# Two-layer block after attention: the channel matrix decoded in the token stage, and layer 1's tensor-tensor work on VectorE

## The chip, the cores and the metric

The kernel runs on one core of a Trainium2 chip. Its engines are TensorE (PE in the views; PEld is its loading of weights), VectorE (DVE), ScalarE (ACT), GpSimd (POOL) and SyncE (SP), which here issues the transfers. The metric is the device time of one execution in microseconds, as the median of several.

## The reference

Three layers in a row, for 4 batches of 448 tokens and 768 channels:

```
attn_out = attention with two 12x12 mixings of the heads      # 4 x 12 x 448 x 64
x = attn_out as (batch, 448, 768)
# layer 1
h = gelu(x @ w_in);  u, v = halves of h                       # 512 columns each
v_n = (v - mean) / sqrt(var + 1e-6) * g_ln
gated = u * (w_sg @ v_n + b_sg)                               # over tokens
x = x + gated @ w_out
# layer 2
theta = x @ w_theta
y = w_tok_r @ (x * cos(theta)) + w_tok_i @ (x * sin(theta))   # over tokens
u = x + y
out = u + relu(u @ w_ch)
```

The weight matrices `w_in`, `w_out`, `w_theta`, `w_tok` and `w_ch` arrive as 64-bit floating-point words.

## The kernel before

Attention takes the first half of the time, in 180 blocks of ten rows and twelve heads. Then two dense layers follow, `moe1` and `moe2`. All their products run in a 32-bit format of reduced precision, three per product: each operand is kept as a high part (a cast, on ScalarE) and a low part (the difference between value and cast, `rest`), and high x high, high x low and low x high are added up in PSUM.

A 64-bit weight has first to be decoded into such a pair. A decode job does it for 128x256 words in six steps: load the raw words (SyncE), *words* (two activations on ScalarE; a shift L602 and a bit operation L604 on VectorE), *value* (a mask, L610, VectorE), *high* (a cast on ScalarE and a product, L618), *low* (a difference L624 and a sum L625, both GpSimd), *store* to DRAM. `tick` issues one step each of several jobs, a later step for an older job. In layer 1 the jobs for `w_out` stay on the chip (tiles named wout); those of `w_theta`, `w_tok` and `w_ch` go to DRAM and are loaded again as pairs when layer 2 needs them. The last 18 jobs are those of `w_ch`.

The order of the work is written out by the kernel itself: a list of *units*, each the products for one PSUM bank, and what stands before and after each unit (`pre`, `post`). Each engine runs its instructions in that order. Units of layer 1 are value chunks (`v_chunk`, 3 or 4 per batch), `out` (6 per batch), `u_half` (4) and `gate` (4). The tables TV, TU, TG and TO say how many ticks stand behind each unit of each kind. The E_ tables choose VectorE (V) or GpSimd (P) for differences and products: of x (E_X), of the normalised v (E_VN), of the gate (E_G), the gate's own product (E_GM), and the product in the decode (E_MV).

In layer 2 a *theta* unit makes half a chunk of angles; `angles` (five instructions on VectorE, three on ScalarE) makes cosine and sine, `rotate` multiplies x by them (two or four on VectorE) and splits the results into z (cast on ScalarE, difference on GpSimd). When the four chunks of batch 0 and the first of batch 1 are through, six token units (`tok`, some 84 products each) follow, each with the addition of x on VectorE (L1092), a cast on ScalarE and a difference on GpSimd (u). Then theta for the rest of batch 1, then six channel units (`ch`) with `w_ch`, and so on through the batches. PSUM is a pool of eight banks that the units take in turn; a transposed x also takes a bank.

Of the kernel before, what the change touches and what calls it, by code (L numbers as in the profile page):

```python
# [18 lines left out]
DM = H * D  # L19
# [458 lines left out]
NO2 = 3  # L478
E_MV = 'PVPPV'
E_X = ('VVVPPP', 'VPVVVP', 'VVPVPP', 'VVVPPP')  # L480
E_VN = ('PPV', 'PPP', 'PPV', 'PVV')
E_GM = ('VVVV', 'VVVV', 'VVVP', 'VVVV')
E_G = ('PPPV', 'VVPP', 'VPVP', 'VVPV')
TV = ((0, 1, 3, 1), (2, 2, 2, 2), (2, 1, 2, 2), (0, 1, 2, 0))
TU = ((2, 1, 0, 1), (2, 0, 2, 1), (2, 0, 2, 1), (3, 0, 2, 1))
TG = ((1, 0, 1, 0), (2, 1, 0, 1), (0, 1, 0, 1), (0, 1, 0, 0))
TO = ((2, 1, 1, 0, 1, 1), (0, 1, 0, 0, 2, 0), (0, 1, 1, 0, 0, 1), (0, 1, 1, 3, 2, 2))
KE = 1
# [8 lines left out]
class Dense:  # L497


    def __init__(self, tc, nc, io, xT, x2T, outT):  # L500
        self.tc, self.nc, self.io = tc, nc, io
        self.xT, self.x2T, self.outT = xT, x2T, outT
        self.pools, self.psum = {}, None
        self.units, self.before, self.after, self.at = [], {}, {}, 0
        self.jobs, self.job_at = [], 0
        self.raw_bufs, self.mid_bufs, self.out_bufs = 1, 1, 1
        self.const = {}
        self.made = 0

# [41 lines left out]

    def eng(self, c):
        return self.nc.vector if c == "V" else self.nc.gpsimd


# [10 lines left out]
    def scratch(self, dram):  # L566
        t = lambda name, r, c: dram.tile([2, r, c], F32, name=name)
        self.win_d = t("win_d", DM, DFF)
        self.wth_d = t("wth_d", DM, DM)
        self.wtok_d = t("wtok_d", 2 * S, S)  # L570
        self.wch_d = t("wch_d", DM, DM)

    def decode(self, src, n, dst, tiles=None):
# [39 lines left out]
        def high(pool):  # L613
            h = block(pool, 0)
            nc.scalar.activation(out=h, in_=box["a"], func=AF.Copy)
            self.made += 1
            eng = self.eng(E_MV[self.made % len(E_MV)]) if not tiles else nc.vector
            eng.tensor_tensor(out=box["p"], in0=box["p"], in1=box["low"], op=ALU.mult)  # L618
            box["h"] = h

        def low(pool):
            a, p, h = (box[k] for k in ("a", "p", "h"))
            lo = block(pool, 1)
            nc.gpsimd.tensor_tensor(out=a, in0=a, in1=h.bitcast(F32), op=ALU.subtract)  # L624
            nc.gpsimd.tensor_tensor(out=lo, in0=a, in1=p, op=ALU.add)  # L625
            box["lo"] = lo
# [37 lines left out]
def moe1(d, left, right):  # L664
# [6 lines left out]
    def start():  # L671
# [21 lines left out]
        for k in range(KF):  # L693
            def tiles(k=k):
# [52 lines left out]
    def split_x(b, k):  # L747
        if k == 0:
            xt[b] = ([], [])
        raw = res.pop(("x", b, k))  # L750
        n = 512 if b % 2 == 0 else S
        h, l = (d.pools["x"].tile([128, 512], F32R, tag=f"x{i}{k}", name="x") for i in range(2))
        d.cast(h[:, :n], raw[:, :n])
        d.rest(d.eng(E_X[b][k]), l[:, :n], raw[:, :n], h[:, :n])
        xt[b][0].append(h)
        xt[b][1].append(l)
# [33 lines left out]
    def norm_split(b, c):  # L790
        v = vraw.pop((b, c))
        if c < 3:
            hi, lo = (d.pools["vn"].tile([128, HF], F32R, tag=f"vn{c}{i}", name="vn") for i in range(2))
            d.cast(hi, v)
            d.rest(d.eng(E_VN[b][c]), lo, v, hi)
            vn[b, c] = (hi, lo)
        else:
            for e in range(2):
                m = d.pools["vn"].tile([128, HF], F32R, tag=f"vnm{e}", name="vnm")
                p, o = slice(64 * e, 64 * e + 64), slice(64 - 64 * e, 128 - 64 * e)  # L800
                d.cast(m[p], v[p])
                d.rest(nc.gpsimd, m[o], v[p], m[p])
                mixed[b + e] = (m, p)
# [16 lines left out]
    def gate(b, f):  # L820
# [6 lines left out]
        for c in range(3):  # L827
# [120 lines left out]
def moe2(d, left, win_es, last_u, m1_left):  # L948
# [301 lines left out]
```

## Time and profile before

| | us |
|---|---|
| median of 3 runs | 1045.97 |
| lowest and highest | 1043.34, 1046.72 |
| the profiled execution, its own time | 1047.47 |
| its span | 1045.6 |
| attention ends and layer 1 begins | about 484 to 531 |
| layer 1 ends, theta begins | 748.3 |
| batch 0's token units begin, end | 785.5, 811.9 |

The span is what the views show; 1.9 us of the execution lie outside it. Times in the views count from the span's start. A lower number in the column of the granted clock (PEclk) means that TensorE ran part of that stretch at 1.2 GHz in place of 2.4. In a row of the timeline the bracket tells how long the engine was idle before and what released it; in a row of grouped lines "mean ns" is the mean length of one instruction.

### The profile page before, as it was taken

What the parts mean: (1) busy time and instruction counts of PE and PEld (TensorE: products, weight loads), DVE (VectorE), ACT (ScalarE), POOL (GpSimd) and SP (SyncE); (2) the same over time, 40 slices, a digit from 0 to 9 for tenths busy, and PEclk for the clock granted to TensorE, in tenths of its full rate; (3) what the DMA queues carried; (4) which work ended last, traced back from release to release, by engine and by line L of the source; (5) the groups of instructions that cost most, each with busy time, mean ns of one, the idle gap of its engine ahead of it and who ended that gap; (6) DMA issues with size and microseconds to landing.
All of it is one profiled execution on the core that took longest, in us unless ns stands there. A gap on an engine that the chain in (4) does not pass through costs nothing.

```text
span 1045.6 us, 21830 instructions
## 1 busy us (share of the span) xinstructions
PE 982.3 (94%) x7848; PEld 742.7 (71%) x7848; DVE 775.5 (74%) x1458; ACT 586.6 (56%) x1374; POOL 622.4 (60%) x818
## 2 busy tenths in 40 slices
PE   7789999999999999997978999799999999999998
PEld 2445655565656555566756979587888999999997
DVE  2799878987888878985989998898896724925611
ACT  4577778786777778775754645454364412613310
POOL 0596558754686548854656877775666643753622
PEclk9899999999999999998989999999999999999999
DMA  5757565556556564347353676758956131130021
GB/s 191 154 167 221 142 139 183 180 168 129 161 193 203 131 158 152 131 108 265 113 155 89 213 225 199 229 188 274 335 184 226 41 106 31 32 106 16 31 76 53
DMA packets 135504, 159.47 MB, mean 153 GB/s; under 512 B 30309, under 2 KB 120933, under 8 KB 135397
## 3 DMA queue, kind: packets, MB, share of 16 engines
q1 hardware_dynamic: 135397, 158.08, 50.3%
q8 instruction: 63, 1.03, 0.4%
q14 instruction: 44, 0.36, 0.1%
HBM read 86.66 MB, written 32.85 MB: 114 GB/s over the span
## 4 chain that ended last, share of the span: by engine, by line
PE 57%; DVE 20%; DMA 9%; POOL 5%; issue 4%; ACT 3%; SPq 1%; DVEq 0%; ACTq 0%; POOLq 0%
PE ps L564 27%; PE psB L223 10%; PE psA L203 5%; PE psD L329 5%; DVE da L604 3%; PE psC L280 3%; PE psC L277 3%; DMA blk<-s 2%; PE psC L278 2%; DVE pl L262 2%; DVE da L602 2%; DVE dp L610 2%; DMA xres<-xT 2%; DVE dp L618 2%; DMA xraw<-xT 1%
## 5 line engine op out<-in xcount | busy, mean ns | idle before, releaser
L255 POOL TENSOR_SCALAR ph<-e,rc 120x448 f16<-120x448 f32 x180 | 163.9, 911 | 147.3 <-DVE rc L250 99.8
L223 PE MATMUL psB<-blk,kpre 120*120 120x448 f32 x360 | 177.3, 575 | 13.0 <-DMA blk<-s 8.2
L229 DVE TENSOR_REDUCE nmx<-psB 120x1 f32<-120x448 f32 x180 | 111.3, 618 | 49.9 <-PE psB L223 40.8
L262 DVE SCALAR_TENSOR_TENSOR pl<-e,rc,ph 120x448 f16<-120x448 f32 x180 | 147.4, 819 | 0.0
L236 ACT ACTIVATE e<-psB,nmx 120x448 f32<-120x448 f32 x180 | 114.3, 635 | 43.1 <-DVE nmx L229 43.0
L308 DVE SCALAR_TENSOR_TENSOR al<-psC,ah 128x480 f16<-128x480 f32 x180 | 116.1, 645 | 8.2 <-ACT ah L302 7.9
L277 PE MATMUL psC<-wh,ph 120*128 120x120 f16 x720 | 97.7, 218 | 10.9 <-DVE al L308 7.1
L302 ACT ACTIVATE ah<-psC 128x480 f16<-128x480 f32 x180 | 103.0, 572 | 7.6 <-PE psC L280 4.9
L209 ACT ACTIVATE s<-psA 120x896 f32<-120x896 f32 (+1 forms) x90 | 82.5, 917 | 42.5 <-PE psA L203 41.1
L564 PE MATMUL ps<-wtok,z 128*128 128x448 f32 x504 | 104.8, 368 | 0.4 <-POOL z L560 0.4
L564 PEld LDWEIGHTS ps<-wtok,z 128*128 128x128 f32 x504 | 94.4, 188 | 10.1 <-POOL z L560 0.8
L277 PEld LDWEIGHTS <-ph 120*128 120x128 f16 x720 | 68.8, 99 | 44.3 <-issue 18.6
L278 PE MATMUL psC<-wl,ph 120*128 120x120 f16 x720 | 97.1, 218 | 2.4 <-issue 2.4
L329 PEld LDWEIGHTS <-ah 128*128 128x128 f16 x1536 | 76.6, 99 | 31.2 <-issue 31.2
L203 PE MATMUL psA<-k,q 64*120 64x448 f32 (+1 forms) x384 | 96.2, 580 | 1.0 <-ACT s L209 1.0
L564 PE MATMUL ps<-wth,x2s 128*128 128x384 f32 x504 | 92.5, 338 | 2.0 <-POOL x2s L560 2.0
L564 PE MATMUL ps<-u,wch 128*128 128x448 f32 x432 | 89.9, 368 | 0.0
L564 PEld LDWEIGHTS ps<-wth,x2s 128*128 128x128 f32 x504 | 87.2, 188 | 2.8 <-POOL x2s L560 2.6
L560 POOL TENSOR_TENSOR z<-zz,z 128x384 fp32r<-128x384 f32 x56 | 61.9, 1125 | 45.8 <-ACT z L557 45.8
L564 PEld LDWEIGHTS ps<-u,wch 128*128 128x128 f32 x432 | 81.0, 188 | 8.1
L278 PEld LDWEIGHTS <-ph 120*128 120x128 f16 x720 | 71.2, 99 | 14.4 <-issue 14.2
L329 PE MATMUL psD<-vl,ah 128*128 128x64 f16 x768 | 78.0, 194 | 1.1 <-POOL vl L185 1.1
(124 smaller groups left out, 2171.9 us busy)
## 6 DMA issues: line engine op xcount, KB each, us to landing
blk<-s SPq DMA_DIRECT2D x176, 210.0 KB
draw<-in_w_in SPq DMA_DIRECT2D x24, 256.0 KB
vraw<-in_vN SPq DMA_DIRECT2D x24, 256.0 KB
k<-in_kvT SPq DMA_DIRECT2D x24, 224.0 KB
vT<-in_kvT SPq DMA_DIRECT2D x12, 448.0 KB
xraw<-xT SPq DMA_DIRECT2D x24, 224.0 KB
xres<-xT SPq DMA_DIRECT2D x24, 224.0 KB
x2T<-xres SPq DMA_DIRECT2D x24, 224.0 KB
```

The lines of the kernel that those rows point to most:

```text
L203: nc.tensor.matmul(ps[e][:n, :S], q[p, o:o + n], k[p], start=True, stop=True)
L223: nc.tensor.matmul(ps[:r, :S], kpre[:r, :r], sblk.pop(s)[:r], start=True, stop=True)
L229: nc.vector.tensor_reduce(out=m[:r], in_=mix[s][:r, :S], axis=AX.X, op=ALU.max, negate=True)
L236: nc.scalar.activation(out=e[:r], in_=mix.pop(s)[:r, :S], func=AF.Exp, bias=nmx.pop(s)[:r], accum_out=sm[:r])
L255: nc.gpsimd.tensor_scalar(out=p[:r], in0=ex[s][0][:r], scalar1=rec[s][:r], scalar2=0.0, op0=ALU.mult, op1=ALU.add)
L262: nc.vector.scalar_tensor_tensor(out=p[:r], in0=ex.pop(s)[0][:r], scalar=rec.pop(s)[:r], in1=ph[s][:r], op0=ALU.mult, op1=ALU.subtract)
L277: nc.tensor.matmul(ps[:, jc, :, :n], cols(a, jc), wh[:r, :, :n], start=(jc == 0), stop=False)
L278: nc.tensor.matmul(ps[:, jc, :, :n], cols(a, jc), wl[:r, :, :n], start=False, stop=False)
L302: nc.scalar.activation(out=at_view(s, at[b, t][0]), in_=src, func=AF.Copy, scale=2.0 ** -17)
L308: nc.vector.scalar_tensor_tensor(out=al, in0=src, scalar=2.0 ** -17, in1=ah, op0=ALU.mult, op1=ALU.subtract)
L329: nc.tensor.matmul(ps[:, o:o + 64], a[:, i0:i0 + 128], v[:, jc, 64 * e:64 * e + 64], start=(o == 0 and m == 0), stop=(o == 320 and m == le ...
L564: self.nc.tensor.matmul(ps, l, r, start=(i == 0), stop=(i == len(terms) - 1))
```

## The change

1. The jobs of `w_ch` are gone from layer 1, with the DRAM pair that they wrote. In layer 2 the raw 64-bit words of `w_ch` are loaded, in twelve tiles of 128x384 (`load_wch`), two with each unit from the fourth last before the token units. `words_wch` and `split_wch` decode a tile: one activation on ScalarE and four instructions on VectorE, and one unit later a cast on ScalarE and two instructions on VectorE. Two tiles' words stand behind the unit before the first token unit and behind each of the first five token units, and their splits one unit later. Scratch is taken from the two tags (zz0, zz1) that `rotate` uses.
2. The E_ tables are gone. The differences of x, normalised v and gate, the gate's product, and the decode's product and difference are all on VectorE. GpSimd keeps the decode's last sum.
3. The tick tables are new, for 18 jobs fewer, mostly one tick to a unit.

```diff
-E_MV = 'PVPPV'
-E_X = ('VVVPPP', 'VPVVVP', 'VVPVPP', 'VVVPPP')
...
-TV = ((0, 1, 3, 1), (2, 2, 2, 2), (2, 1, 2, 2), (0, 1, 2, 0))
...
+TV = ((), (2, 2, 2), (1, 1, 1, 1), (1, 1, 1))
+TU = ((2, 1, 1, 1), (1, 1, 1, 1), (1, 1, 1, 1), (1, 1, 1, 1))
...
         def high(pool):
...
-            eng = self.eng(E_MV[self.made % len(E_MV)]) if not tiles else nc.vector
-            eng.tensor_tensor(out=box["p"], in0=box["p"], in1=box["low"], op=ALU.mult)
+            nc.vector.tensor_tensor(out=box["p"], in0=box["p"], in1=box["low"], op=ALU.mult)
...
-            nc.gpsimd.tensor_tensor(out=a, in0=a, in1=h.bitcast(F32), op=ALU.subtract)
+            nc.vector.tensor_tensor(out=a, in0=a, in1=h.bitcast(F32), op=ALU.subtract)
             nc.gpsimd.tensor_tensor(out=lo, in0=a, in1=p, op=ALU.add)
...
-                   + d.decode_all(io["w_tok"], 0, S, d.wtok_d)
-                   + d.decode_all(io["w_ch"], 0, DM, d.wch_d))
+                   + d.decode_all(io["w_tok"], 0, S, d.wtok_d))
...
-        d.rest(d.eng(E_X[b][k]), l[:, :n], raw[:, :n], h[:, :n])
+        d.rest(nc.vector, l[:, :n], raw[:, :n], h[:, :n])
...
     def load_wch(k, half):
-        wch[k, half] = d.load_pair(d.pools["wch"], d.wch_d, slice(128 * k, 128 * k + 128),
-                                   slice(384 * half, 384 * half + 384), f"wch{k}_{half}")
+        raw = d.pools["wch"].tile([128, 384, 2], U32, tag=f"wch{k}_{half}", name="wchraw")
+        src = io["w_ch"][128 * k:128 * k + 128, 384 * half:384 * half + 384]
+        nc.sync.dma_start(out=raw.rearrange("p n w -> p (n w)"), in_=src.bitcast(U32))
+        wch[k, half] = raw
+
+    def words_wch(k, half):
+        raw = wch[k, half]
+        a, p = (d.pools["t2"].tile([128, 384], F32, tag=f"zz{i}", name=f"ch{i}") for i in range(2))
+        nc.scalar.activation(out=p, in_=raw[:, :, 1].bitcast(F32), func=AF.Copy, scale=2.0 ** -112)
+        au, pu = a.bitcast(U32), p.bitcast(U32)
+        nc.vector.tensor_scalar(out=au, in0=pu, scalar1=3, scalar2=0x7FFFFFF8,
+                                op0=ALU.logical_shift_left, op1=ALU.bitwise_and)
+        nc.vector.scalar_tensor_tensor(out=au, in0=pu, scalar=0x80000000, in1=au,
+                                       op0=ALU.bitwise_and, op1=ALU.bitwise_or)
+        nc.vector.tensor_scalar(out=pu, in0=au, scalar1=0xFF800000, scalar2=None, op0=ALU.bitwise_and)
+        nc.vector.tensor_tensor(out=p, in0=p, in1=raw[:, :, 0], op=ALU.mult)
+        st["ch", k, half] = a, p
+
+    def split_wch(k, half):
+        a, p = st.pop(("ch", k, half))
+        t = d.pools["wch"].tile([128, 2, 384], F32R, tag=f"wch{k}_{half}", name="wch")
+        d.cast(t[:, 0], a)
+        d.rest(nc.vector, a, a, t[:, 0])
+        nc.vector.scalar_tensor_tensor(out=t[:, 1], in0=p, scalar=2.0 ** -52, in1=a, op0=ALU.mult, op1=ALU.add)
+        wch[k, half] = t[:, 0], t[:, 1]
...
-    for k in range(KD):
-        for half in range(2):
-            d.pre(tok0 + k, load_wch, k, half)
+    for half in range(2):
+        for k in range(KD):
+            i = tok0 - 1 + (KD * half + k) // 2
+            d.pre(i - 2, load_wch, k, half)
+            d.post(i + 1, split_wch, k, half)
+    for half in range(2):
+        for k in range(KD):
+            d.post(tok0 - 1 + (KD * half + k) // 2, words_wch, k, half)
```

VectorE's order where the gate matrix (wsg) and the normalised v (vn) of batch 0 are split, in the kernel before (da, dp and dl are a decode job's tiles; line numbers of the two kernels differ by some ten):

```order
L787 TENSOR_SCALAR v<-v,mv,sd 128x512 x2
L560 TENSOR_TENSOR wsg<-wsgraw,wsg 128x448 x2
L618 TENSOR_TENSOR dp<-dp,dl 128x256
L610 TENSOR_SCALAR dp<-da 128x256
L602 TENSOR_SCALAR da<-dp 128x256
L604 SCALAR_TENSOR_TENSOR da<-dp,da 128x256
```

The same place in the changed kernel, where a job's difference also has a row (da<-da,wout):

```order
L774 TENSOR_SCALAR v<-v,mv,sd 128x512 x2
L551 TENSOR_TENSOR wsg<-wsgraw,wsg 128x448 x2
L551 TENSOR_TENSOR vn<-v,vn 128x512 x2
L606 TENSOR_TENSOR dp<-dp,dl 128x256
L600 TENSOR_SCALAR dp<-da 128x256
L592 TENSOR_SCALAR da<-dp 128x256
L594 SCALAR_TENSOR_TENSOR da<-dp,da 128x256
L612 TENSOR_TENSOR da<-da,wout_9959 128x256
```

Two differences of vn came from GpSimd to VectorE, and each job takes five instructions of VectorE in place of four (or three).

VectorE's order around batch 0's token units before: the angles of the first chunk of batch 1, the six token additions (xres), and the products that rotate that chunk (zz):

```order
L1042 TENSOR_SCALAR n<-ps 128x384
L1043 TENSOR_SCALAR n<-n 128x384
L1045 SCALAR_TENSOR_TENSOR r<-n,ps 128x384
L1046 SCALAR_TENSOR_TENSOR r<-n,r 128x384
L1047 TENSOR_SCALAR r<-r 128x384
L1092 TENSOR_TENSOR xres<-ps,xres 128x448 x6
L1069 TENSOR_TENSOR zz<-ps,n 128x384
L1069 TENSOR_TENSOR zz<-ps,r 128x384
```

The same place in the changed kernel, up to the second pair of tiles (ch_ are the scratch tiles of the decode, wch the finished pair):

```order
L1057 SCALAR_TENSOR_TENSOR r<-n,r 128x384
L1058 TENSOR_SCALAR r<-r 128x384
L1103 TENSOR_TENSOR xres<-ps,xres 128x448
L551 TENSOR_TENSOR ch_12661<-ch_12661,wch 128x384
L985 SCALAR_TENSOR_TENSOR wch<-ch_12662,ch_12661 128x384
L551 TENSOR_TENSOR ch_12668<-ch_12668,wch 128x384
L985 SCALAR_TENSOR_TENSOR wch<-ch_12669,ch_12668 128x384
L972 TENSOR_SCALAR ch_12726<-ch_12727 128x384
L974 SCALAR_TENSOR_TENSOR ch_12726<-ch_12727,ch_12726 128x384
L976 TENSOR_SCALAR ch_12727<-ch_12726 128x384
L977 TENSOR_TENSOR ch_12727<-ch_12727,wchraw 128x384
```

Four more such rows of words follow for the pair's second tile, then the second addition. Eight rows of words for the first pair stand ahead of the angles. Each of the six additions is followed by four split rows, and each of the first five also by eight rows of words.

ScalarE's order at the same place in the changed kernel (L970 is the words' activation, n and r the angles' sine and cosine):

```order
L970 ACTIVATE ch_12662<-wchraw 128x384
L970 ACTIVATE ch_12669<-wchraw 128x384
L1059 ACTIVATE n<-r 128x384
L1060 ACTIVATE n<-n,hpi 128x384
L1061 ACTIVATE r<-r 128x384
L548 ACTIVATE u<-xres 128x448
L548 ACTIVATE wch<-ch_12661 128x384
L548 ACTIVATE wch<-ch_12668 128x384
L970 ACTIVATE ch_12727<-wchraw 128x384
L970 ACTIVATE ch_12734<-wchraw 128x384
L548 ACTIVATE u<-xres 128x448
```

Before, the six casts of u stood in a row here; now a pair's two casts stand behind each cast of u.

## Rows read from the trace of the kernel before

**Rows 1.** Page, part 1: busy us (share of the span) xinstructions.

```profile
PE 982.3 (94%) x7848; PEld 742.7 (71%) x7848; DVE 775.5 (74%) x1458; ACT 586.6 (56%) x1374; POOL 622.4 (60%) x818
```

**Rows 2.** TensorE's waits from 440 us: us in total, times, longest.

```profile
PE ps L564 <- DVE wsg L560: 3.4, 1, 3.4
PE ps L564 <- POOL wout L625: 3.3, 1, 3.3
```

**Rows 3.** Table of units: length, busy (instructions) by engine, granted clock, DMA share, GB/s.

```profile
531.20:551.80 20.60, 14.42 (x46) 9.57 (x44) 20.36 (x28) 11.52 (x29) 15.02 (x15) 0.75 0.31 95
599.30:609.80 10.50, 10.50 (x46) 7.87 (x45) 8.98 (x14) 5.58 (x13) 9.07 (x10) 1.00 0.86 261
564.50:577.20 12.70, 9.38 (x38) 8.03 (x37) 12.42 (x28) 7.27 (x19) 10.12 (x13) 0.87 0.59 184
592.00:599.50 7.50, 7.50 (x38) 6.96 (x38) 7.33 (x12) 4.49 (x14) 7.19 (x10) 1.00 0.87 267
667.40:689.00 21.60, 16.81 (x56) 11.84 (x56) 19.30 (x31) 7.88 (x20) 15.67 (x17) 0.84 0.64 199
551.80:564.60 12.80, 12.76 (x56) 10.24 (x56) 12.63 (x20) 6.34 (x17) 8.91 (x9) 1.00 0.19 49
721.20:748.30 27.10, 24.44 (x109) 21.34 (x109) 20.56 (x34) 9.62 (x22) 14.20 (x17) 0.94 1.05 362
```

**Rows 4.** The same table, layer 1 and the token stage.

```profile
500.00:748.00 248.00, 227.92 (x1125) 190.99 (x1124) 218.31 (x367) 129.66 (x319) 175.62 (x198) 0.95 0.64 200
...
785.00:826.00 41.00, 40.59 (x216) 37.99 (x215) 27.18 (x46) 17.84 (x37) 24.61 (x23) 1.00 0.51 165
```

**Rows 5.** VectorE by line, 500 to 748 us: busy us, mean ns, idle before.

```profile
L604 DVE SCALAR_TENSOR_TENSOR da<-dp,da 128x256 uint32<-128x256 uint32 x61 | 50.4, 826 | 2.1
...
L602 DVE TENSOR_SCALAR da<-dp 128x256 uint32<-128x256 uint32 x61 | 31.8, 521 | 6.2 <-ACT dp L599 6.2
L618 DVE TENSOR_TENSOR dp<-dp,dl 128x256 f32<-128x256 f32 x37 | 27.6, 746 | 0.0
```

**Rows 6.** VectorE's timeline in layer 1: start us, us, line, operation.

```profile
566.67 0.39 DVE L618 TENSOR_TENSOR dp<-dp,dl 128x256 f32<-128x256 f32 x1
...
567.50 0.83 DVE L604 SCALAR_TENSOR_TENSOR da<-dp,da 128x256 uint32<-128x256 uint32 x1
...
569.32 0.28 DVE L602 TENSOR_SCALAR da<-dp 128x256 uint32<-128x256 uint32 x1
...
655.79 0.42 DVE L604 SCALAR_TENSOR_TENSOR da<-dp,da 128x256 uint32<-128x256 uint32 x1
```

**Rows 7.** VectorE's timeline in the token stage.

```profile
791.81 0.36 DVE L1047 TENSOR_SCALAR r<-r 128x384 f32<-128x384 f32 x1
...
793.83 0.56 DVE L1065 TENSOR_TENSOR zz<-ps,r 64x384 f32<-64x384 f32 x1
...
795.55 0.56 DVE L1045 SCALAR_TENSOR_TENSOR r<-n,ps 128x384 f32<-128x384 f32 x1
...
796.84 1.05 DVE L1047 TENSOR_SCALAR r<-r 128x384 f32<-128x384 f32 x1
797.82 1.14 DVE L1092 TENSOR_TENSOR xres<-ps,xres 128x448 f32<-128x448 f32 x2
...
803.60 0.62 DVE L1092 TENSOR_TENSOR xres<-ps,xres 128x448 f32<-128x448 f32 x1 [3.63 <-PE ps L564]
```

**Rows 8.** GpSimd and ScalarE in the same stage.

```profile
796.36 2.42 POOL L560 TENSOR_TENSOR x2s<-x,x2s 128x384 fp32r<-128x384 f32 x2
...
804.26 0.58 ACT L557 ACTIVATE u<-xres 128x448 fp32r<-128x448 f32 x1 [3.34 <-DVE xres L1092]
804.91 1.15 POOL L560 TENSOR_TENSOR u<-xres,u 128x448 fp32r<-128x448 f32 x1 [1.48 <-ACT u L557]
```

**Rows 9.** TensorE's timeline after the token units.

```profile
811.91 3.31 PE L564 MATMUL ps<-wth,x2s 128*128 128x384 f32 x18
...
822.56 3.39 PE L564 MATMUL ps<-wth,x2s 128*128 128x384 f32 x18
```

More of the change, by code (lines that the diff above doesn't have):

```diff
@@ L478 @@
 NO2 = 3
-E_MV = 'PVPPV'
-E_X = ('VVVPPP', 'VPVVVP', 'VVPVPP', 'VVVPPP')
-E_VN = ('PPV', 'PPP', 'PPV', 'PVV')
-E_GM = ('VVVV', 'VVVV', 'VVVP', 'VVVV')
-E_G = ('PPPV', 'VVPP', 'VPVP', 'VVPV')
-TV = ((0, 1, 3, 1), (2, 2, 2, 2), (2, 1, 2, 2), (0, 1, 2, 0))
-TU = ((2, 1, 0, 1), (2, 0, 2, 1), (2, 0, 2, 1), (3, 0, 2, 1))
-TG = ((1, 0, 1, 0), (2, 1, 0, 1), (0, 1, 0, 1), (0, 1, 0, 0))
-TO = ((2, 1, 1, 0, 1, 1), (0, 1, 0, 0, 2, 0), (0, 1, 1, 0, 0, 1), (0, 1, 1, 3, 2, 2))
+TV = ((), (2, 2, 2), (1, 1, 1, 1), (1, 1, 1))
+TU = ((2, 1, 1, 1), (1, 1, 1, 1), (1, 1, 1, 1), (1, 1, 1, 1))
+TG = ((1, 0, 1, 0), (1, 0, 1, 0), (1, 0, 1, 0), (1, 0, 0, 0))
+TO = ((1, 1, 1, 1, 1, 0), (1, 0, 1, 0, 1, 0), (1, 0, 1, 0, 1, 0), (0, 0, 0, 0, 0, 0))
 KE = 1
@@ L507, in __init__ @@
         self.const = {}
-        self.made = 0
     def unit(self, fn, *a):
@@ L550, in stage @@
         return self.pools["st"].tile([128, 512], F32, tag="st", name=name)[:, :n]
-    def eng(self, c):
-        return self.nc.vector if c == "V" else self.nc.gpsimd
     def cast(self, out, in_):
@@ L570, in scratch @@
         self.wtok_d = t("wtok_d", 2 * S, S)
-        self.wch_d = t("wch_d", DM, DM)
     def decode(self, src, n, dst, tiles=None):
@@ L615, in high @@
             nc.scalar.activation(out=h, in_=box["a"], func=AF.Copy)
-            self.made += 1
-            eng = self.eng(E_MV[self.made % len(E_MV)]) if not tiles else nc.vector
-            eng.tensor_tensor(out=box["p"], in0=box["p"], in1=box["low"], op=ALU.mult)
+            nc.vector.tensor_tensor(out=box["p"], in0=box["p"], in1=box["low"], op=ALU.mult)
             box["h"] = h
@@ L794, in norm_split @@
             d.cast(hi, v)
-            d.rest(d.eng(E_VN[b][c]), lo, v, hi)
+            d.rest(nc.vector, lo, v, hi)
             vn[b, c] = (hi, lo)
@@ L801, in norm_split @@
                 d.cast(m[p], v[p])
-                d.rest(nc.gpsimd, m[o], v[p], m[p])
+                d.rest(nc.vector, m[o], v[p], m[p])
                 mixed[b + e] = (m, p)
@@ L835, in gate @@
                                        op0=ALU.mult, op1=ALU.add)
-        d.eng(E_GM[b][f]).tensor_tensor(out=t, in0=t, in1=uT[b][f], op=ALU.mult)
+        nc.vector.tensor_tensor(out=t, in0=t, in1=uT[b][f], op=ALU.mult)
         res["g", b, f] = t
@@ L842, in gate_split @@
         d.cast(h, t)
-        d.rest(d.eng(E_G[b][f]), l, t, h)
+        d.rest(nc.vector, l, t, h)
         gt[b][0].append(h)
```

## The prediction

> **What bounds the kernel now.** I read the page first, then TensorE's waits from the end of attention on, then tables by stage, then single instructions. The page says that TensorE is busy 94% of the span and VectorE 74% [rows 1]; an average over three parts says little here, so the stages decide. TensorE's waits after 500 us are few and mostly in the first dense layer: 3.4 us for the gate matrix's second term from VectorE, 3.3 us for a `w_out` tile that GpSimd finishes [rows 2]. The cost of such a wait is larger than the wait, because TensorE afterwards runs at a lower granted clock. The table of units shows it [rows 3]. The first gate units of batch 0 took 20.6 us, at a mean granted clock of 0.75 of full speed; batch 1's, at 1.00, took 10.5. The first three output units took 12.7 us, the same work later 7.5. The value units of batch 3 took 21.6 us, batch 1's 12.8. The last six output units and three of the batch before took 27.1 us, where three times 7.5 is 22.5. That is 10.1 + 5.2 + 8.8 + 4.6 = 28.7 us. With some 4 us of smaller waits, in the gates of batch 2 and in the theta stage, it makes 33 us that could come back at most. In the second layer from 785 us on TensorE is never short of work: 40.59 of 41.0 us in the token stage [rows 4]. VectorE has room there: 27.18 of 41, and it sits idle 3.63 us in front of a token addition until TensorE has finished [rows 4, 7].
>
> **First part: VectorE takes GpSimd's work in layer 1, and the channel jobs leave.** From 500 to 748 us VectorE is busy 218.3 us and GpSimd 175.6 of 248 [rows 4]. Much of VectorE's time is waiting inside its own instructions. A decode shift (L602) takes 0.28 us undisturbed, a multiplication (L618) 0.39, the two-operand bit operation (L604) 0.42; with GpSimd at work the last takes 0.83 [rows 6]. Their means from 500 to 748 us are 521, 746 and 826 ns [rows 5]; the mask (L610), of one operand and as many instructions, I take like the shift. So the decode groups hold 61 x 0.40 + 2 x 61 x 0.24 + 37 x 0.36 = 67 us above their undisturbed length. Added to VectorE there: about 50 decode subtractions and 19 multiplications at 0.39 us (those of GpSimd without the channel matrix's), and 8 differences of x, 12 of the normalised v, 8 of the gate and one gate product, 29 at 0.62 (an addition of 448 columns [rows 7]) to 0.70 (the same for 512, by width): 19.5 + 7.5 + 19.6 = 46.6 us. Removed: 17 channel jobs x 1.14 us (0.28 + 0.42 + 0.28, and two in five times 0.39) = 19.4. GpSimd keeps some 40 us (a final addition for each of about 50 jobs, and the first x2s), so the 67 us shrink in proportion, 67 x 40/176 = 15, a saving of 52. VectorE's load becomes 218 + 46.6 - 19.4 - 52 = 193 us.
>
> That is an average again. By stretches, counting instructions at their uncontended length: from the first gate unit to batch 1's, VectorE had 41 us and gets 55, against 53 us of clean TensorE work; from there to batch 2's gates 38 becomes 46 against 57; to batch 3's 27 becomes 29 against 45. So the first stretch stays bound by VectorE and the later ones stop being so. For the first I walked VectorE's queue forward: gate matrix and v tiles ready at about 536.6 instead of 540.2, the last `w_out` tile at 565.5 instead of 570.2, so 4.5 us of 15.3 come back. Of batch 2's gates and batch 3's value units (10.2 us) I take 9.5, since nothing but VectorE, GpSimd and a DMA behind two jobs issued in one unit stood there and the jobs are now one to a unit; of the last output units 3.3 of 4.6, of theta 0.7 of 2.5. Sum: 18 us. Bounds: 5 (only what the walk of the first stretch gives) and 33 (all). The changed jobs during attention add 14 subtractions and some multiplications to VectorE, about 9 us over 400, and take 20 us from GpSimd; I count this as nothing, hidden in waits, with 2 us either way.
>
> The Trainium skill (SBUF — State Buffer, Who interferes with whom) says that VectorE and GpSimd contend over one shared pair of ports, that an instruction of VectorE with two SBUF inputs is affected, and that the loser blocks outright. The trace agrees (0.42 against 0.83 us [rows 6]). Followed to its end the rule speaks for more than my 18 us: with GpSimd nearly silent the collisions all but vanish. That case is the second rival.
>
> **Second part: the channel matrix in the token stage.** Removed are 18 loads, 18 stores and 12 reloads; TensorE waits for none of them, so I count nothing. The raw loads that come instead are as large as the reloads were and are issued two units before their use, in a stage whose transfers fill half of the DMA engines' time (0.51 [rows 4]): nothing either. Added are twelve tiles of 128x384, two behind each of six units: per tile on VectorE a shift, a bit operation, a mask and a product (words), and one unit later a difference and a final sum (split), with a conversion and a cast on ScalarE. For 384 columns a one-operand instruction takes 0.36 us and a two-operand one 0.56 when undisturbed; under GpSimd's work 1.05 for the former [rows 7], which I take as the upper end for the latter too. A tile's words are 0.36 + 0.56 + 0.36 + 0.54 = 1.82 us and its split 0.53 + 0.56 = 1.09; twelve make 35 us. The idle VectorE had there is 41 - 27 = 14 us, so it cannot swallow them, and 35 - 14 = 21 us is the plain estimate of what is late.
>
> What counts is the queue. Before, six token additions stood in a row; now between two additions VectorE has two splits and two words. And a split waits: its cast stands on ScalarE behind the cast of the addition's own result (0.58 us [rows 8]) and takes 0.5 itself by width, so VectorE sits about 1.1 us after each addition with eight word instructions queued behind. GpSimd's difference of u (1.15 us [rows 8]) then runs beside the first split and costs it about 0.55. A round is 0.62 (addition) + 1.1 + 0.55 + 2 x 1.09 + 2 x 1.82 = 8.1 us, where TensorE delivers a unit in 0.62 + 3.63, some 4.3 [rows 7]. The first round starts late as well: the rotation before it ends at 794.4 [rows 7], the first two words beside GpSimd's z and x2s differences (2.42 us for two [rows 8]) take 5 us, the angles of the next half 2.5 to 3.5, so the first addition is at about 803 instead of 798, the sixth at about 845 instead of 812, the last splits end at 849.5 and the two rotation products at 850.5.
>
> TensorE cannot run ahead, since PSUM has eight banks, used in turn. It finishes the six token units on time at 811.9 [rows 9]. The next chunk's theta matmuls need the bank that the first addition frees, its transposes those of the second and third, the following half the fourth's, and so on; the last theta half needs the angles of the half two before it, which stand on VectorE behind every split and rotation. So this half, which ran from 822.6 to 825.9 [rows 9], starts at about 852 and ends at 855.3: 29 us late. Then the channel products follow; VectorE has room again and the rest is shifted. From below: with no waiting and no contention VectorE has 44 us of work from 793.4 to those angles (35 for the channel matrix, 2.4 and 1.6 for angles, 3.7 for additions, 1.1 for a rotation), which gives 15 us late; from above: rounds of 9.3 us give 36. I take 29, the walked value, as both the 1.1 and the 0.55 rest on rows. TensorE is interrupted for some 35 us, and in the interrupted units of layer 1 the granted clock was 0.75 to 0.94 [rows 3]; the last theta half and the first channel unit at half speed would cost 4 us; I take 2.
>
> **Sum.** Against the profiled execution (span 1045.6, 1.9 us outside it, 1047.5): 1047.5 - 18 + 29 + 2 = 1060.5. The median of the runs shown is 1.5 us lower, so 1059.
>
> **Rivals.**
> The other side: the token stage hides the decode. One mechanism, the banks: if TensorE's order or the release of banks leaves it enough room, or if ScalarE's cast is early enough and the rounds fit in about 5 us, the additions keep within 4 us of TensorE and the loss is under 4. Then it is 1046 - 18 + 2 = 1030. For it speaks that VectorE is idle for 14 us of the stage [rows 4]; against it that 35 us of work stand between the rotation and the last theta half. It decides where a round is under 5.5 us. Chance 0.08.
> Layer 1 gives back all, as the port rule would have it: 33 instead of 18, and the loss of 31 stays: 1046 - 33 + 31 = 1044 to 1049, no change. For it: 67 us of collisions [rows 5, 6]. Against it: the first stretch has 55 us of VectorE work for 53 of TensorE's even without any. Chance 0.11.
> Layer 1 stays bound by VectorE: gain 5, loss 31: 1046 + 26 = 1072. For it: the 46.6 us added; against it, VectorE's 193 of 248. Chance 0.10.
> My forecast, gain 10 to 25 and loss 22 to 36 with clock: 1047 to 1069. Chance 0.71.
>
> **How the numbers follow.** Measured differences under 0.3% (3 us, so 1042.8 to 1049.1) can't be told from none. Faster: 0.08 of the first rival, 0.04 of the second (a loss at its lower bound of 15 with a gain above it, which would also do). Same: 0.07 of the second and 0.02 of the forecast's lower edge, 0.09. Slower: the rest, 0.79. The range that leaves out 2 in 10 goes from 1044 to 1071: below lie the first rival and a little of the second, above the slowest third of the third and walks worse than mine.
>
> **What would show it.** In the changed profile TensorE should wait in 812 to 855 (in its own later or earlier time, after layer 1's gain) some 25 to 30 us in four to six pieces, released by token additions and the angles; VectorE should be without idle time there except 1 us behind each addition, released by ScalarE's cast; a round should be near 8 us. In layer 1 the first gate units should take some 17 us, batch 3's value units under 14, and the bit operation's mean should fall from 826 ns towards 500. The prediction is wrong if rounds are near 5 us, or if TensorE's theta halves don't wait.

## Result and the profile after

The changed kernel takes 1059.8 us (median of 4, 1057.68 to 1063.52), the kernel before 1045.9 (4 runs): 1.013 times as long, 95% interval 1.0093 to 1.0168. The profiled execution took 1061.3 us with a span of 1059.3. The forecast was 1059, from 18 us gained in layer 1 and 31 lost in the token stage.

The stages, read from where TensorE begins each kind of unit in the two traces, and in the experiments below (us):

| kernel | median (ratio to before, interval) | first gate to theta | theta to tokens | tokens to first channel unit | behind that |
|---|---|---|---|---|---|
| before | 1045.9 | 217.1 | 37.2 | 40.3 | 219.8 |
| changed | 1059.8 (1.0093 to 1.0168) | 201.0 | 36.6 | 73.3 | 218.7 |
| e1, no channel decode | 1025.5 (0.9788 to 0.9833) | 199.3 | 38.4 | 39.9 | 219.6 |
| e2, casts first | 1053.1 (1.0059 to 1.0109) | 198.4 | 38.6 | 65.6 | 219.6 |
| e3, second half late | 1052.6 (1.0060 to 1.0094) | 200.3 | 38.9 | 51.7 | 236.4 |
| e6, engines of before | 1060.7 (1.0135 to 1.0166) | 200.5 | 36.8 | 72.6 | 219.6 |
| e11, old ticks | 1063.8 (1.0149 to 1.0235) | 207.0 | 38.2 | 71.6 | 219.6 |
| e5, VectorE only | 1034.5 (0.9887 to 0.9919) | 210.5 | 38.0 | 40.3 | 220.0 |
| e10, new ticks alone | 1045.4 (1.0000 to 1.0037) | 206.3 | 46.4 | 40.7 | 220.2 |
| e4, channel in layer 1 | 1039.5 (0.9942 to 0.9978) | 205.8 | 43.8 | 40.3 | 220.2 |
| e7, the same, spread | 1041.4 (0.9955 to 1.0004) | 210.2 | 45.7 | 39.9 | 220.2 |
| e8, half and half | 1036.4 (0.9906 to 0.9946) | 198.7 | 39.3 | 51.5 | 219.5 |
| e9, one unit later | 1035.3 (0.9905 to 0.9954) | 196.3 | 39.8 | 50.1 | 219.6 |

The intervals are against the kernel before as it was timed along with each run (median 1043.2 to 1044.0 there, 1045.9 beside the changed kernel), so kernels are compared by them and not by the medians alone.

The first gate unit itself begins between 522.8 and 531.6 us, in kernels with the same attention too (526.9 and 529.6 for e1 and the changed one), so the total of one execution is not the sum of effects to a microsecond. Layer 1 scatters too. Four kernels have the same layer 1, the changed one, e1, e2 and e3: from the first gate unit to the end of the first three output units (called the first stretch below) they take 40.8 to 43.7 us, where the kernel before took 46.0. Behind that they repeat, 157.3 to 157.6 us up to theta, where the kernel before took 171.1. Their theta stages take 36.6 to 38.9.

The page after, part 1 (as [rows 1]; busy us, share, instructions). GpSimd has lost 147 us; TensorE's work is the same:

```profile
PE 983.0 (93%) x7848; PEld 747.9 (71%) x7848; DVE 784.2 (74%) x1596; ACT 581.1 (55%) x1344; POOL 475.1 (45%) x644
```

TensorE's waits from 440 us on (as [rows 2]: total, times, longest). The gate matrix's wait is gone from 3.4 to 0.3; the `w_out` tile's stands. New and largest are waits for token additions (L1103), by theta products (L555) and by transposes (L1042): these wait for the PSUM banks that the additions free.

```profile
PE ps L555 <- DVE xres L1103: 10.2, 2, 7.2
PE ps L1042 <- DVE xres L1103: 8.5, 2, 6.6
...
PE ps L1042 <- issue: 4.3, 1, 4.3
PE ps L555 <- POOL wout L613: 3.1, 1, 3.1
...
PE ps L555 <- DVE wsg L551: 0.3, 1, 0.3
```

The table of units (as [rows 3]): gates of batch 0, first output units, value units of batch 3, last nine output units; then layer 1 from the first gate unit, and the token stage to the first channel unit (columns as there).

```profile
529.60:545.80 16.20, 13.04 (x46) 9.09 (x45) 15.92 (x37) 12.93 (x32) 3.79 (x5) 0.89 0.44 139
561.10:573.40 12.30, 9.16 (x38) 8.03 (x37) 12.06 (x31) 7.15 (x16) 3.90 (x6) 0.86 0.53 163
661.70:674.20 12.50, 12.50 (x56) 10.31 (x56) 12.16 (x28) 5.74 (x14) 2.17 (x3) 1.00 0.45 138
706.50:730.70 24.20, 22.78 (x110) 20.17 (x110) 8.94 (x15) 5.46 (x10) 4.23 (x4) 1.00 0.55 166
529.60:730.60 201.00, 190.91 (x861) 162.18 (x861) 159.09 (x353) 94.70 (x217) 41.04 (x48) 0.98 0.58 183
767.30:840.70 73.40, 48.86 (x212) 44.30 (x211) 61.64 (x112) 26.70 (x55) 20.96 (x21) 0.79 0.20 69
```

Against [rows 3] the four became 4.4, 0.4, 9.1 and 2.9 us shorter, 16.8 in all. In the token stage VectorE is busy 61.6 of 73.4 us and the granted clock is 0.79, where it was 1.00 before [rows 4].

VectorE's timeline in one round of the token stage (as [rows 7]: start, length, line, then idle time and what ended it). The first round takes 9.09 us, since VectorE waits 2.00 us there for ScalarE's cast. From the second addition on they stand 8.13 us apart, and behind each VectorE waits 1.06 us for the cast; the first difference is stretched from 0.55 to 1.19 us beside GpSimd. The last rows are the sixth addition and the second product of the rotation behind it:

```profile
786.00 0.62 DVE L1103 TENSOR_TENSOR xres<-ps,xres 128x448 f32<-128x448 f32 x1
788.62 1.20 DVE L551 TENSOR_TENSOR ch<-ch,wch 128x384 f32<-128x384 f32 x1 [2.00 <-ACT wch L548]
...
795.09 0.62 DVE L1103 TENSOR_TENSOR xres<-ps,xres 128x448 f32<-128x448 f32 x1
796.77 1.19 DVE L551 TENSOR_TENSOR ch<-ch,wch 128x384 f32<-128x384 f32 x1 [1.06 <-ACT wch L548]
...
798.47 0.55 DVE L551 TENSOR_TENSOR ch<-ch,wch 128x384 f32<-128x384 f32 x1
...
803.23 0.62 DVE L1103 TENSOR_TENSOR xres<-ps,xres 128x448 f32<-128x448 f32 x1
...
827.63 0.62 DVE L1103 TENSOR_TENSOR xres<-ps,xres 128x448 f32<-128x448 f32 x1
...
832.52 0.55 DVE L1080 TENSOR_TENSOR zz<-ps,r 128x384 f32<-128x384 f32 x1
```

TensorE's timeline behind the token units (as [rows 9]), which ended at 793.7:

```profile
796.84 0.49 PE L1042 MATMUL ps<-ident,x 128*128 128x128 f32 x3
803.90 0.90 PE L1042 MATMUL ps<-ident,x 128*128 128x128 f32 x3 [6.58 <-DVE xres L1103]
812.03 5.28 PE L555 MATMUL ps<-wth,x2s 128*128 128x384 f32 x18 [7.22 <-DVE xres L1103]
820.25 6.10 PE L555 MATMUL ps<-wth,x2s 128*128 128x384 f32 x18 [2.95 <-DVE xres L1103]
828.30 0.55 PE L1042 MATMUL ps<-ident,x 128*128 128x128 f32 x3 [1.95 <-DVE xres L1103]
833.17 0.87 PE L1042 MATMUL ps<-ident,x 128*128 128x128 f32 x3 [4.32 <-issue]
835.15 5.63 PE L555 MATMUL ps<-wth,x2s 128*128 128x384 f32 x18 [1.11 <-DVE r L1056]
```

The first four of these waits end 0.7 us after an addition begins (803.23 and 803.90). The wait that the view puts down to "issue" ends at 833.17, 0.1 us behind the end of the rotation's product (832.52 and 0.55); in e2, e8 and e9 the same wait also ends 0.1 us behind that product, so it is VectorE's queue again. A theta half of 3.3 us takes 5.3 to 6.1 at the lower clock.

### The profile page after: what moved, and what is told of

Read it like the earlier page. It is cut to its first block, busy times and chain, and to the rows that moved or that the text cites. A ratio compares the mean times of both kernels' runs of the same rounds, so it can differ in the third digit from the quotient of the medians.

```text
span 1059.3 us, 21638 instructions
## 1 busy us (share of the span) xinstructions
PE 983.0 (93%) x7848; PEld 747.9 (71%) x7848; DVE 784.2 (74%) x1596; ACT 581.1 (55%) x1344; POOL 475.1 (45%) x644
## 4 chain that ended last, share of the span: by engine, by line
PE 68%; DVE 16%; DMA 6%; ACT 4%; issue 3%; POOL 2%; SPq 0%; DVEq 0%; ACTq 0%; POOLq 0%
PE ps L555 38%; PE psB L223 10%; PE psA L203 6%; PE psD L329 5%; DMA blk<-s 3%; PE psC L277 3%; PE psC L280 3%; DVE pl L262 2%; PE psC L278 2%; DVE al L308 1%; DVE nmx L229 1%; DMA wchraw<-in_w_ch 1%; DVE ch L551 1%; PE psT L342 1%; DVE dp L606 1%
## 5 line engine op out<-in xcount | busy, mean ns | idle before, releaser
L255 POOL TENSOR_SCALAR ph<-e,rc 120x448 f16<-120x448 f32 x180 | 173.9, 966 | 158.2 <-DVE rc L250 107.2
L229 DVE TENSOR_REDUCE nmx<-psB 120x1 f32<-120x448 f32 x180 | 111.2, 618 | 46.7 <-PE psB L223 39.8
L262 DVE SCALAR_TENSOR_TENSOR pl<-e,rc,ph 120x448 f16<-120x448 f32 x180 | 143.5, 797 | 0.0
L555 PE MATMUL ps<-wth,x2s 128*128 128x384 f32 x504 | 99.3, 355 | 13.0 <-DVE xres L1103 10.2
L555 PE MATMUL ps<-wtok,z 128*128 128x448 f32 x504 | 104.3, 367 | 0.4 <-POOL z L551 0.4
L555 PEld LDWEIGHTS ps<-wth,x2s 128*128 128x128 f32 x504 | 93.8, 201 | 14.5 <-DVE xres L1103 7.6
L555 PEld LDWEIGHTS ps<-wtok,z 128*128 128x128 f32 x504 | 94.5, 188 | 9.5 <-POOL z L551 0.8
L555 PE MATMUL ps<-u,wch 128*128 128x448 f32 x432 | 89.5, 367 | 0.0
L555 PEld LDWEIGHTS ps<-u,wch 128*128 128x128 f32 x432 | 81.1, 188 | 7.6
L613 POOL TENSOR_TENSOR dh<-da,dp 128x256 fp32r<-128x256 f32 (+1 forms) x46 | 37.0, 803 | 95.1 <-DVE da L612 57.6
```

The costliest lines, as they stand in the source:

```text
L229: nc.vector.tensor_reduce(out=m[:r], in_=mix[s][:r, :S], axis=AX.X, op=ALU.max, negate=True)
L255: nc.gpsimd.tensor_scalar(out=p[:r], in0=ex[s][0][:r], scalar1=rec[s][:r], scalar2=0.0, op0=ALU.mult, op1=ALU.add)
L262: nc.vector.scalar_tensor_tensor(out=p[:r], in0=ex.pop(s)[0][:r], scalar=rec.pop(s)[:r], in1=ph[s][:r], op0=ALU.mult, op1=ALU.subtract)
L555: self.nc.tensor.matmul(ps, l, r, start=(i == 0), stop=(i == len(terms) - 1))
```

## The experiments

**The token stage.** e1 leaves the decode of the channel matrix out:

```diff
-        raw = d.pools["wch"].tile([128, 384, 2], U32, tag=f"wch{k}_{half}", name="wchraw")
...
+        wch[k, half] = d.load_pair(d.pools["wch"], d.wth_d, slice(128 * k, 128 * k + 128),
+                                   slice(384 * half, 384 * half + 384), f"wch{k}_{half}")
...
-            d.post(i + 1, split_wch, k, half)
...
-            d.post(tok0 - 1 + (KD * half + k) // 2, words_wch, k, half)
```

> The changed kernel without the channel matrix's decode: the pair of w_theta is loaded in its place, so the channel product has the wrong weights. Theory (the loss sits in VectorE's queue in the token stage, 33 us between the start of theta and the last theta half of batch 1): 1060 - 33 = 1027, 1023 to 1031, and TensorE busy without a break from the token units to the channel units. Rival (part of the loss is the raw loads or something behind the stage): 1035 or more.

Measured: 1025.5 us, the stage 39.9 in place of 73.3. TensorE's timeline there has no bracket left:

```profile
790.64 3.29 PE L555 MATMUL ps<-wth,x2s 128*128 128x384 f32 x18
793.77 0.82 PE L1040 MATMUL ps<-ident,x 128*128 128x128 f32 x6
794.35 6.51 PE L555 MATMUL ps<-wth,x2s 128*128 128x384 f32 x36
```

The whole loss is the decode's. e1 loads pairs of the same size in place of the raw words, so the raw loads are not separated from the decode. No wait of TensorE, VectorE or ScalarE in the changed kernel's stage is put down to one; the chain of its page (part 4) passes through two of them, which landed at 776.6, 0.9 us before the first activation of the decode.

e2 takes the wait behind each addition away: the casts go ahead of it in ScalarE's queue.

```diff
+    def cast_wch(k, half):
...
+        d.cast(t[:, 0], a)
...
     def split_wch(k, half):
-        a, p = st.pop(("ch", k, half))
...
-        d.cast(t[:, 0], a)
...
+            d.post(tok0 - 1 + (KD * half + k) // 2, cast_wch, k, half)
```

> The changed kernel with ScalarE's casts of a channel pair ahead of the token addition's cast, so that VectorE needn't wait behind an addition. Theory (a round is VectorE's work plus 1.06 us of wait): rounds fall from 8.13 to about 7.1, the sixth addition comes 6 to 7 us sooner, 1053 to 1054. Rival (rounds are set by something else, a bank or a load): rounds stay 8.1, 1060.

Measured: 1053.1 us, the stage 65.6, 7.7 less. VectorE's timeline of a round:

```profile
788.84 0.62 DVE L1107 TENSOR_TENSOR xres<-ps,xres 128x448 f32<-128x448 f32 x1
789.38 0.55 DVE L551 TENSOR_TENSOR ch<-ch,wch 128x384 f32<-128x384 f32 x1
...
790.44 1.52 DVE L551 TENSOR_TENSOR ch<-ch,wch 128x384 f32<-128x384 f32 x1
...
796.17 0.62 DVE L1107 TENSOR_TENSOR xres<-ps,xres 128x448 f32<-128x448 f32 x1
```

The wait is gone and the round is 7.33 us; 0.8 of 1.06 came back, since GpSimd's difference now falls on an instruction that it stretches by 0.97. That shows the wait of 1.1 us as a term of the round. The 0.55 us for the meeting with GpSimd was not taken away by any run; it measured 0.64 in the changed kernel and 0.97 here.

e3 decodes the second half of the tiles behind theta units:

```diff
...
+    for k in range(KD):
+        d.post(tok0 - 1 + k // 2, words_wch, k, 0)
+    for f in (words_wch, split_wch):
+        for k in range(KD):
+            d.post(tok0 + 7 + k // 2, f, k, 1)
```

> The changed kernel with the second half of the channel tiles decoded behind theta units of batch 1 in place of the last three token units. Theory (TensorE's theta waits for the banks that the additions free; VectorE's whole work until the fourth channel unit counts): theta units wait far less, the last theta half ends some 25 us sooner than in the changed kernel, but the channel products then wait for the second half: 10 us gained, 1045 to 1055. Rival (place doesn't matter, the sum of VectorE's work up to there does): no gain, 1058 to 1062.

Measured: 1052.6 us. The first channel unit comes 21.6 us sooner, as the theory of the banks said, but the channel units now wait for VectorE: 5.7 us for the angles of theta (L1056), of which the first row shows 3.29, and 6.4 for the second half itself (TensorE's timeline):

```profile
832.42 3.96 PE L555 MATMUL ps<-u,wch 128*128 128x448 f32 x12 [3.29 <-DVE r L1056]
841.15 0.74 PE L555 MATMUL ps<-u,wch 128*128 128x448 f32 x1 [4.77 <-ACT wch L548]
843.53 10.19 PE L555 MATMUL ps<-u,wch 128*128 128x448 f32 x41 [1.63 <-DVE wch L985]
```

The part behind takes 17.7 us more (236.4 against 218.7). The total lies in the theory's range, but by stages 3.9 of the expected 10 us remain, nearer to the rival. So in this other place most of the loss stays: VectorE's work up to the last channel tile has to be done, and the banks mostly say where the wait for it shows.

**Layer 1.** e6 is the changed kernel with layer 1's work on the engines of before:

```diff
+E_MV = 'PVPPV'
+E_X = ('VVVPPP', 'VPVVVP', 'VVPVPP', 'VVVPPP')
...
-            nc.vector.tensor_tensor(out=a, in0=a, in1=h.bitcast(F32), op=ALU.subtract)
+            nc.gpsimd.tensor_tensor(out=a, in0=a, in1=h.bitcast(F32), op=ALU.subtract)
```

> The changed kernel with layer 1's work on the engines of before (GpSimd takes its share of differences and products), channel matrix in the token stage, ticks of the change. Theory (by my sum VectorE's load is 178 to 193 either way): theta begins within 4 us of the changed kernel's 730.7, 1056 to 1064. Rival (moving the work is what gave the gain): theta begins at about 745, 1072 to 1076.

Measured: 1060.7 us, theta at 730.4. Layer 1 of e6 (columns of the table of units) against that of the changed kernel above:

```profile
529.60:730.60 201.00, 190.47 (x864) 161.44 (x863) 154.30 (x259) 91.87 (x211) 125.97 (x140) 0.98 0.58 183
```

GpSimd is busy 126 us in place of 41, VectorE 154 in place of 159, and TensorE as before. Its decode instructions collide as they did in the kernel before, 780 ns for the bit operation (VectorE by line):

```profile
L603 DVE SCALAR_TENSOR_TENSOR da<-dp,da 128x256 uint32<-128x256 uint32 x43 | 33.5, 780 | 1.5
```

So in the changed kernel the move from GpSimd is worth nothing in time (layer 1 takes 200.5 us without it, 201.0 with it), and the collisions that it takes away cost nothing there. e5 makes this move alone, in the kernel before:

```diff
-        d.rest(d.eng(E_X[b][k]), l[:, :n], raw[:, :n], h[:, :n])
+        d.rest(nc.vector, l[:, :n], raw[:, :n], h[:, :n])
...
-            nc.gpsimd.tensor_tensor(out=a, in0=a, in1=h.bitcast(F32), op=ALU.subtract)
+            nc.vector.tensor_tensor(out=a, in0=a, in1=h.bitcast(F32), op=ALU.subtract)
```

> The kernel before with one part of the change: all tensor-tensor work of layer 1 on VectorE, channel jobs and ticks as before. Theory (my sum: VectorE's load 218 + 46.6 + 7 more subtractions and a few products - the collisions, about 222 of 248): gain 0 to 5 us, 1041 to 1046. Rival (the collisions with GpSimd are the whole of layer 1's stalls): gain 15, about 1031.

Measured: 1034.5 us, between the two, and 9.3 below the kernel before as timed along with it (1043.8), more than my 0 to 5. By stages layer 1 gains 6.6 us. The rest stands ahead of it, in an attention that ended at 467.1 us in this trace and at 475.6 in that of the kernel before. So the move helps with the old ticks. With the new ticks and all jobs in layer 1 (e10 and e4 below, which differ by the move alone) it is worth 0.5 us in layer 1 and 2.6 in theta.

e10 and e11 swap the tick tables (the numbers per unit alone):

```diff
-TV = ((0, 1, 3, 1), (2, 2, 2, 2), (2, 1, 2, 2), (0, 1, 2, 0))
+TV = ((), (2, 2, 2), (1, 1, 1, 1), (1, 1, 1))
...
```

> The kernel before with one part alone: tick tables that are the changed kernel's up to batch 2, with the 18 channel jobs behind batch 3's last u, gate and output units; engines as before. Theory (the long value units of batch 3 came from two jobs to a unit): these units take 12.5 us in place of 21.6, the last nine output units about 33 in place of 27.2, so layer 1 from the first gate unit to theta 212 to 216 in place of 217.1; 1041 to 1046. Rival (GpSimd's share of the work made them long): they stay above 18 us.

> The changed kernel with the tick tables of before (its 55 jobs in layer 1 are used up earlier). Theory (ticks matter, the jobs' number too): batch 3's value units 14 to 18 us, layer 1 from the first gate unit to theta 204 to 208 in place of 201; 1062 to 1067. Rival (fewer jobs are the whole gain): 201 as before, 1059 to 1061.

Measured: 1045.4 and 1063.8 us. The value units of batch 3, then e10's last nine output units (table of units); first e10, then e11:

```profile
662.10:674.60 12.50, 12.50 (x56) 10.36 (x56) 11.07 (x21) 5.63 (x14) 8.41 (x10) 1.00 0.48 146
706.80:738.00 31.20, 25.06 (x110) 21.73 (x110) 22.73 (x41) 9.73 (x26) 18.37 (x22) 0.89 0.97 334
```

```profile
656.90:675.10 18.20, 14.77 (x56) 11.40 (x56) 16.72 (x38) 6.04 (x15) 3.03 (x4) 0.91 0.49 162
```

With the old engines and the new ticks these units take 12.5 us; with the new engines and the old ticks 18.2, just above my 14 to 18. So the ticks give the 9 us of batch 3 (21.6 to 12.5) whatever the engines; the move alone gives 3 of them (18.4 in e5). e10's layer 1 was shorter than expected (206.3), because its gates and first output units gained too, and gave 9.2 us back in theta, where the last of the late jobs ran. As a whole it is not faster than the kernel before (1.0000 to 1.0037).

Layer 1 and theta together show what the gain is made of. The ticks alone (the kernel before and e10) give 1.6 us, the absence of the 18 jobs alone (e5 and e11) 3.3. Both together, with the engines of before (the kernel before and e6), give 17.0, and the changed kernel has 16.7. The two pay together and hardly at all apart.

**Where else the channel matrix could go.** e4 puts the 18 jobs back into layer 1, in the last units; e7 spreads them.

```diff
-TU = (..., (1, 1, 1, 1))
+TU = (..., (2, 2, 2, 2))
...
-TO = (..., (1, 0, 1, 0, 1, 0), (0, 0, 0, 0, 0, 0))
+TO = (..., (1, 0, 1, 1, 1, 1), (2, 2, 1, 2, 2, 0))
```

> The changed kernel with the channel matrix decoded in layer 1 again, 18 jobs in the last units (second half of batch 3's u, gates, last output units), all on VectorE but for the last sum. VectorE has 33 us idle from 680 to 740 us in the changed kernel, 18 jobs need 18 x 1.76 = 32 us. Theory (layer 1's gain comes from freeing the earlier stretches): most of the 18 us stay, 1030 to 1036. Rival (the gain is only the 18 jobs fewer): it is given back, 1042 to 1048.

> The channel matrix in layer 1 on VectorE as in the run before, but its 18 jobs spread: none behind batch 3's gates, six in earlier value and u units, nine behind the last output units. Theory (what that run lost, 8.5 us in the last nine output units and 6.6 in theta, came from decode jobs queued ahead of gate differences): the output units take 25 to 27 us in place of 32.9, 1031 to 1035. Rival (VectorE simply has too little room for 18 jobs): 1038 to 1042.

Measured: 1039.5 and 1041.4 us. e4 lies between theory and rival, e7 in its rival's range: the last nine output units took 33.0 us, again waiting for gate differences. Its trace shows the rival's reason too. VectorE works through one decode job after another, and the first product of batch 3's gates (L823) comes at 711.18 (698.67 in the changed kernel); of the 20 us from 700 on VectorE is busy 19.55:

```profile
699.57 0.83 DVE L593 TENSOR_SCALAR da<-dp 128x256 uint32<-128x256 uint32 x1
...
701.65 0.83 DVE L593 TENSOR_SCALAR da<-dp 128x256 uint32<-128x256 uint32 x1
...
711.18 0.68 DVE L823 SCALAR_TENSOR_TENSOR gt<-ps,gln,bsg 128x448 f32<-128x448 f32 x1
```

A job takes 2.08 us here, not 1.76, because its shift (0.28 undisturbed) takes 0.83; at that length eighteen would need 37 us and not 32. ScalarE also waits 9.8 us for stores of decoded pairs to leave the job's buffers. These waits are not the cause: they end at 734.56 and 739.35, after the last cast of a gate (719.77), and e8 has 11.3 us of them and loses nothing in layer 1.

e8 puts only half of the matrix there, 12 jobs, and one tile to a token unit, with its cast first; e9 begins these a unit later.

```diff
+                   + d.decode_all(io["w_ch"], 0, 384, d.wch_d))
...
+        d.post(tok0 + k, split_wch, k, 1)
...
+        d.post(tok0 - 1 + k, words_wch, k, 1)
+        d.post(tok0 - 1 + k, cast_wch, k, 1)
```

> Half of the channel matrix as 12 jobs in layer 1's last units, the other half decoded in the token stage, one tile to a unit with its cast ahead of the addition's. Theory (a round is 0.62 + 1.09 + 1.82 + about 0.6 = 4.1 us, under TensorE's 4.3): no wait for banks, loss in the token stage under 4 us, 1027 to 1033. Rival (any decode in the stage delays theta): a loss of half of 33, 1040 or more.

> As the run with half of the channel matrix in layer 1, but the other half's words begin behind the first token unit, not ahead of the angles before it, and its splits stand a unit later each. Theory (the 11 us that run still lost came from a first addition 4.5 us late and rounds of 4.64 against TensorE's 4.35): the first addition comes within 1 us of TensorE, the stage loses 4 to 7 us in place of 11, 1029 to 1033. Rival (the last splits delay batch 1's angles as much): 11 us as before, 1035 to 1037.

Measured: 1036.4 and 1035.3 us. The 12 jobs cost layer 1 nothing (198.7 and 196.3, and 157.3 in both behind the first stretch, as in the changed kernel); the token stage still loses 11.2 and 9.8. VectorE's round of e8:

```profile
785.84 0.62 DVE L1112 TENSOR_TENSOR xres<-ps,xres 128x448 f32<-128x448 f32 x1
786.57 0.56 DVE L551 TENSOR_TENSOR ch<-ch,wch 128x384 f32<-128x384 f32 x1
787.17 1.55 DVE L994 SCALAR_TENSOR_TENSOR wch<-ch,ch 128x384 fp32r<-128x384 f32 x1
...
790.48 0.62 DVE L1112 TENSOR_TENSOR xres<-ps,xres 128x448 f32<-128x448 f32 x1
```

A round is 4.64 us, 0.3 over TensorE's, and the collision takes 0.99 of it. e9's rival was right. Its first addition comes 12.3 us behind the first token unit, as in the kernel before, but the splits that come a unit later delay batch 1's rotation and angles instead: TensorE waits 4.5 and 2.6 us for them. Both kernels, e4 and e5 are faster than the kernel before and the changed one; between e5, e8 and e9 the intervals do not decide.

## Why the prediction was right

**The token stage** came as walked. A round was 8.13 us for 8.1; the first addition stood 18.7 us behind the first token unit for 17.5 (803 less 785.5), the sixth 60.3 for 59.5. The walk has a slip there: five rounds of 8.1 from 803 end at 843.5, not at about 845. It did no harm, by luck, since the first round was 1 us longer than the others: the casts of the first pair stand on ScalarE behind three activations of the angles as well, which the walk left out. (A token unit is 21 products, 126 for the six, not some 84 each as the description above has it; the walk goes by its time and not by this.) The stage grew by 33.0 us for 29 + 2: the additions were about 1 us later still, and the lower clock cost the last theta half 2.2 us (5.63 for 3.39). TensorE waited 24 us in six pieces, for 25 to 30 in four to six, released by additions and angles as written and once, after 4.3 us, by the rotation. e1 shows that the decode is the cause, e2 that the wait of 1.06 us is a term of the round. What e3 corrects is the weight given to the banks: they pass the delay on, and where they did not, the channel units waited for most of the same work.

**Layer 1** gained 16.1 us from the first gate unit to theta and 0.6 in the theta stage (less than its scatter), for a forecast of 18 with both. Batch 2's gates and batch 3's value units gave 10.7 for 9.5, the last output units 2.9 for 3.3. The first stretch gave 2.2 for 4.5 in this trace: its gates and output units gained 4.8, but the value units between them went from 12.7 to 15.3 us. The whole first stretch, before and after (table of units):

```profile
531.20:577.20 46.00, 36.46 (x136) 27.77 (x135) 45.31 (x73) 25.03 (x62) 34.05 (x37) 0.85 0.35 107
529.60:573.40 43.80, 35.14 (x136) 27.18 (x136) 42.93 (x98) 26.20 (x63) 10.20 (x13) 0.92 0.36 109
```

VectorE stays busy nearly throughout, as forecast. But the reason given for the 4.5 us did not hold: e6 and e10, with GpSimd's share as before, take 42.7 and 41.8 us for this stretch, no more than the changed kernel. That this term came out within 3 us is luck.

The mechanism that I put first did not carry the gain: "so the 67 us shrink in proportion, 67 x 40/176 = 15, a saving of 52". The decode groups after (VectorE by line, as [rows 5]):

```profile
L600 DVE TENSOR_SCALAR dp<-da 128x256 uint32<-128x256 uint32 x44 | 24.5, 558 | 0.0
L592 DVE TENSOR_SCALAR da<-dp 128x256 uint32<-128x256 uint32 x43 | 21.3, 495 | 2.5 <-ACT dp L589 2.5
L606 DVE TENSOR_TENSOR dp<-dp,dl 128x256 f32<-128x256 f32 x45 | 18.8, 418 | 0.0
L594 DVE SCALAR_TENSOR_TENSOR da<-dp,da 128x256 uint32<-128x256 uint32 x43 | 18.7, 436 | 1.5
```

The two-operand groups fell from 826 and 746 ns to 436 and 418, below the 500 I named. The shift hardly did (521 to 495), and the mask rose (541 to 558), so some 23 us are left above the undisturbed lengths for the 15 forecast. Each job still has one sum on GpSimd, and the shift or the mask meets it (changed kernel):

```profile
613.85 0.90 POOL L613 TENSOR_TENSOR dh<-da,dp 128x256 fp32r<-128x256 f32 x1 [4.95 <-ACT g L548]
...
614.07 0.83 DVE L592 TENSOR_SCALAR da<-dp 128x256 uint32<-128x256 uint32 x1
```

But e6, with all collisions, has the same layer 1: the saving was real and not on the path. What is left as the cause is the ticks together with the jobs' absence (17.0 us in e6, against 1.6 and 3.3 apart). That "the jobs are now one to a unit" was the reason that held, for 9.5 of the 18 us. It covers the largest term of the sum; the total came near by that and by the luck of the first stretch.

**The rivals.** The decode hidden in the token stage (0.08) fell with the round of 8.13. That layer 1 gives back all its 33 us did not come: the path did not run through the collisions. The Trainium skill (SBUF — State Buffer, Who interferes with whom) says that an instruction of VectorE with two SBUF inputs contends with one of GpSimd that reads SBUF. The trace agrees for the instructions (826 to 436 ns for the bit operation when most of GpSimd's work is gone). That layer 1 stays bound by VectorE did not come either: it is busy 159 of 201 us.

## What to carry to other kernels

Work moved into a stage where an engine idles has to fit between the instructions that others wait for: count the round (work, waits for other engines' queues, collisions) against the pace of the engine that it serves, and then ask until when the last result is needed. Contention that a profile shows is worth what the path pays for it; here 15 us of stretching in the bit operations alone (43 x 0.34) were worth nothing in the changed kernel, while the same move was worth 6.6 us of layer 1 under the old ticks. Two parts of a change can each be worth little and much together, as the ticks and the jobs' absence were, so a part is worth testing both in the kernel before and in the kernel after. A kernel that is freed in one place should be timed by stages, and the scatter of each stage taken from kernels that have the same code there, since an early stage's scatter can be as large as the effect.

## What the runs showed that I had not expected

A one-operand instruction of VectorE (0.28 us for 256 columns) is stretched to 0.83 by a single GpSimd instruction of 0.90 that reads two operands, and a two-operand one of 384 columns from 0.56 to 1.55 beside one of 1.16. So one badly placed GpSimd instruction cost VectorE 0.55 of 0.90 us and 0.99 of 1.16, most of its own length. And the end of attention scatters: in the ten traces of kernels with VectorE's decode in attention its last block's score product ends between 466.1 and 473.1 us, in the three with GpSimd's share at 472.3, 475.2 and 475.6. The means are 469.6 and 474.4. So a few microseconds of the move may lie there, where I had counted nothing; three traces against ten that spread over 7 us do not settle it.
